# Keys and queries of the last six quads: transposed by DMA, scored in 64-row tiles

## The chip, the core and the metric

The kernel runs on one core of a Trainium2 chip. Its engines work beside each other and meet through semaphores: PE (matrix multiplies, with its weight loads listed as PEld), DVE (VectorE), ACT (ScalarE), POOL (GpSimd) and SP, which here issues DMAs only. POOL issues DMAs as well. The metric is the device time of one execution in microseconds. Before the change it is 323.39 us, the median of three runs (322.47 to 325.67).

## The reference

Attention with a decay per token, for 8 batches of 8 heads, 576 tokens, head dimension 64; its output is then put through a two-layer network with a tanh gelu.

```
scores = q @ k.T / sqrt(64)                      # per batch and head, 576 x 576
cum    = cumsum(log(clip(f, 1e-4, 1)))           # f: batch x head x token
attn   = softmax(where(causal, scores + cum_q - cum_k, -1e9))
x      = attn @ v      -> 4608 tokens x 512      # heads side by side
out    = gelu_tanh(x @ w_in) @ w_out             # 512 -> 2048 -> 512, float32 out
```

All inputs are float32 in HBM.

## The kernel before

**Quads.** Attention goes by quads of four heads of one batch: 16 quads, numbered i = 0 to 15, batch i // 2. Everything that belongs to quad i lies in buffer i % 2 of a pair. For a quad, `load_one` brings keys and queries from HBM with one DMA each, issued by POOL, which also makes bfloat16 of them (`k_c`, `q_c`: 32 partitions a head, each with 18 tokens of 64). `transpose_words` then has DVE transpose them in 32x32 blocks of 32-bit words, so that a word holds two neighbouring elements of the head dimension: `kT` and `qT` have 32 partitions for each of the four heads, and the two elements (c = 0, 1) side by side.

**Scores.** `scores(i, r)` makes round r (of three) of a quad's scores, transposed: keys on partitions, queries along the columns, only those at or under the diagonal. The 1536 columns of a quad are cut into pieces of 64 to 448 columns, seven over the three rounds. For each c, piece and head there is one matmul of 32 rows (half of the head dimension), so that four heads run abreast on four row tiles of PE; the second pass, c = 1, is added to the first. Two exponentials on ACT then write `pt`. `mask` (POOL) or `mask_by_product` (DVE) clears what lies above the diagonal.

**Products.** `denominators` (D) sums `pt` with the decay weights, `attn_out` (V) multiplies it by the weighted values `vw`; `make_vw` (VW) makes these from `v_nat`, which `load_v` (LV) brings by five DMAs from SP. The quotient goes to `xT`, the network's input.

**The network.** It goes by chunks of 512 tokens, nine of them, partly by schemes that save one of eight block products (`seven_in`, `seven_products`). Its matmuls fill PE between the steps of attention. Its results are stored from SP, from four staging buffers (`o_st`).

**Order.** There is no planner: the order is written out by hand. `setup()`, then the list `FRONT` (quads 0 to 6 and the first chunks), then `TABLES[c]` for c = 2 to 8, one stage each. Each word is one step: `S.q4.0` is `scores` of quad 2c + 4, round 0; `M`/`m` masks; `D`, `V`, `VW` as above; `cl` a small copy on POOL; `TK`, `TQ` transposes of keys and queries; `LK`, `LQ` their loads; `LV` the loads of values; `P`, `R` first-layer products, `F`, `f`, `O` second-layer ones by so many steps; `G`, `K`, `T` sums on DVE; `X`, `Y` change ACT's table. A step for a quad above 15 is left out. Each engine takes its instructions in this order and waits, in order, for what each one needs; the framework puts the waits in by what each instruction reads and writes. So a step that waits holds all later steps on the same engine, also DMAs that POOL or SP issues.

In stage c the scores made are those of quads 2c + 3 (three rounds) and 2c + 4 (three rounds, the last at the stage's end). Quads 10 and 11 are scored in stages 3 and 4, and the last, 15, in stage 6.

Lines of the profile that matter here: L191 the loads of keys and queries, L168 those of values, L197 DVE's transposes, L260 the score matmuls, L268 the exponentials, L274 POOL's masks, L214 `make_vw`, L219 `cl`, L328 the products D and V, L347 the first step after D, L359 `xT`, L540 and L373 matmuls of the network, L553 the stores.

Of the kernel before, what the change touches and what calls it, by code (L numbers as in the profile page):

```python
# [9 lines left out]
BF16 = mybir.dt.bfloat16  # L10
# [6 lines left out]
def kernel(  # L17
# [10 lines left out]
    nc = tc.nc  # L28

    B, H, S, D = q.shape  # L30
# [13 lines left out]
    NB = S // 64  # L44
# [42 lines left out]
    TABLES[2] = """  # L87
        Y O.512 P.0.1 R.1 P.4.1 R.1 R.1 TK.q3 TQ.q3 LK.q5 LQ.q5 m.q2.1 M.q2.2.2 m.q2.0 m.q2.2.3 CL.q2 LV P.2 G.0 P.3 K.3.0 K.3.1 K.3.2 P.6 P.7 K.3.3
        G.1.1.2 X F.10 S.q3.0 D.q2 M.q3.0 f.22 S.q3.1 V.q2.0 TK.q4 TQ.q4 M.q3.1 VW.q3 f.18 S.q3.2 V.q2.1 M.q3.2 cl.q3 TK.q5 f.16 S.q4.0 VW.q4 cl.q4
        D.q3 M.q4.0 f.18 S.q4.1 TQ.q5 V.q3.0 M.q4.1 f.13 V.q3.1 T f.3 S.q4.2  # L90
    """
    TABLES[3] = """
        Y O.512 LK.q4 LQ.q4 P.0.1 R.1 P.4.1 R.1 R.1 LK.q5 LQ.q5 M.q2.2 LV R.3 P.2.1 R.3 G.0.1.2 P.6 R.3 G.0.3.4 G.1.1.2 X F.10 S.q3.0 D.q2 M.q3.0
        f.22 S.q3.1 V.q2.0 TK.q4 TQ.q4 M.q3.1 VW.q3 f.18 S.q3.2 V.q2.1 M.q3.2 cl.q3 TK.q5 f.16 S.q4.0 VW.q4 cl.q4 D.q3 M.q4.0 f.18 S.q4.1 TQ.q5
        V.q3.0 M.q4.1 f.13 V.q3.1 T f.3 S.q4.2
    """
    TABLES[4] = """
        Y O.512 LK.q4 LQ.q4 P.0.1 R.1 P.4.1 R.1 R.1 LK.q5 LQ.q5 M.q2.2 LV R.3 P.2.1 R.3 G.0.1.2 P.6 R.3 G.0.3.4 G.1.1.2 X F.10 S.q3.0 D.q2 M.q3.0
        f.22 S.q3.1 V.q2.0 TK.q4 TQ.q4 M.q3.1 VW.q3 f.18 S.q3.2 V.q2.1 M.q3.2 cl.q3 TK.q5 f.16 S.q4.0 VW.q4 cl.q4 D.q3 M.q4.0 f.18 S.q4.1 TQ.q5
        V.q3.0 M.q4.1 f.13 V.q3.1 T f.3 S.q4.2  # L100
    """
    TABLES[5] = """
        Y O.512 LK.q4 LQ.q4 P.0.1 R.1 P.4.1 R.1 R.1 LK.q5 LQ.q5 M.q2.2 LV R.3 P.2.1 R.3 G.0.1.2 P.6 R.3 G.0.3.4 G.1.1.2 X F.10 S.q3.0 D.q2 M.q3.0
        f.22 S.q3.1 V.q2.0 TK.q4 TQ.q4 M.q3.1 VW.q3 f.18 S.q3.2 V.q2.1 M.q3.2 cl.q3 TK.q5 f.16 S.q4.0 VW.q4 cl.q4 D.q3 M.q4.0 f.18 S.q4.1 TQ.q5
        V.q3.0 M.q4.1 f.13 V.q3.1 T f.3 S.q4.2
    """
    TABLES[6] = """
        Y O.512 P.0.1 R.1 P.4.1 R.1 R.1 LK.q5 LQ.q5 M.q2.2 LV R.3 P.2.1 R.3 G.0.1.2 P.6 R.3 G.0.3.4 K.0.0 K.0.1 K.0.2 G.1.1.2 X F.10 S.q3.0 D.q2
        M.q3.0 f.22 S.q3.1 V.q2.0 M.q3.1 VW.q3 f.18 S.q3.2 V.q2.1 M.q3.2 cl.q3 f.20 D.q3 f.18 V.q3.0 v.q3.1 T f.14 K.0.3
# [17 lines left out]
    def many(n, shape, dtype, name):  # L127
        return [singles.tile(shape, dtype, name=f"{name}{i}") for i in range(n)]
# [57 lines left out]

    parts = [(0, QA), (QA, S)]

    def load_one(src, dst, i):
        b, h0 = i // QPB, 4 * (i % QPB)  # L190
        return nc.gpsimd.dma_start(  # L191
            out=dst[i % 2].rearrange("p a d -> p (a d)"),
            in_=src[b, h0:h0 + 4].rearrange("h (p a) d -> (h p) (a d)", p=32))

    def transpose_words(src, dst):

        nc.vector.transpose(  # L197
            out=dst.rearrange("p s c -> p (s c)").bitcast(FP32)
                .rearrange("p (t a) -> p a t", a=S // 32),
            in_=src.rearrange("p a d -> p (a d)").bitcast(FP32)  # L200
                .rearrange("p (a d) -> p a d", d=D // 2),
        )

    def transpose_k(i):
# [16 lines left out]
    def key_columns(i, key, h, c):  # L221

        b0 = {"low": 0, 0: 1, 1: 3, 2: 5, 3: 7, "high": NB}[key]
        return kT[i % 2][32 * h:32 * h + 32, 64 * b0:64 * b0 + 128, c]

    def load_exp():

        nc.scalar.activation(spare, shift[0:1, :], AF.Exp)
# [13 lines left out]
    def scores(i, r, groups=((0, 1, 2, 3),)):  # L242

        qq, p = qT[i % 2], pt[i % 2]
        if i < 2:
            off, n = split_rounds[r]
            todo = [(key, col - off, q0, nq) for (key, col, q0, nq) in split_pieces[r]]
        else:
            off, n = rounds[r]
            todo = []  # L250
            for (key, col, q0, nq) in pieces:
                a, z = max(col, off), min(col + nq, off + n)
                if a < z:
                    todo.append((key, a - off, q0 + a - col, z - a))
        for heads in groups:
            tiles = {g: psS.tile([128, 2, 512], FP32, name="ps_s", tag="s") for g in sorted({h // 2 for h in heads})}
            for c in range(2):
                for j, (key, c0, q0, nq) in enumerate(todo):
                    for h in heads:
                        nc.tensor.matmul(  # L260
                            tiles[h // 2][:, h % 2, c0:c0 + nq],
                            key_columns(i, key, h, c),
                            qq[32 * h:32 * h + 32, q0:q0 + nq, c],
                            start=(c == 0 and j == 0), stop=(c == 1),
                            skip_group_check=True,
                        )
            for g, t in tiles.items():
                nc.scalar.activation(p[:, 2 * g:2 * g + 2, off:off + n], t[:, :, 0:n], AF.Exp, scale=scale)  # L268
# [433 lines left out]
    def load_values(b, half):  # L702
# [124 lines left out]
```

## Time and profile before

The profiled execution took 322.39 us; the profile's span of it is 320.7 us. All durations below come from that one execution.

| | |
|---|---|
| median of three runs | 323.39 us |
| profiled execution / its span | 322.39 / 320.7 us |
| PE clock granted | full, all through |
| score matmuls (L260) | 896, in rounds of 16 or 24 |
| DVE transposes of keys and queries (L197) | 32, mean 1.24 us |
| loads of keys and queries (L191) | 32, 0.53 to 0.72 us of POOL each |
| stores (L553, from SP) | 35, median 2.3 us to landing |
| stage 3 / 4 / 5 | 132.3 to 166.0 / 166.0 to 199.6 / 199.6 to 233.3 us |

Idle time on an engine costs nothing unless another waits for it; where an engine is busy all the time, only its own work or what it waits for counts. A time of an instruction on POOL or SP that issues a DMA is the time to issue it; the transfer goes on after that ("to landing").

### The profile page before, as it was taken

Reading aid. Unit: us, or ns where it says so; the run is one execution under the profiler, and the core shown is the slowest. Engines: PE = TensorE matmul, PEld = TensorE weight load, DVE = VectorE, ACT = ScalarE, POOL = GpSimd, SP = SyncE. Lnnn points to the kernel's source line nnn. Section 1 sums busy time; section 2 is a strip of 40 time slices with the busy share of each in tenths; the row PEclk is TensorE's granted clock in tenths of the full one; section 3 lists DMA queues with packets and bytes.
Section 4 is the critical chain, followed back from the end, with each engine's and each line's share of the span. In section 5 each row is a group of like instructions: output and inputs, shape, how many; then the busy total and the mean of one; then the engine's idle time right before and its main releaser. Section 6 shows DMA issues by size and latency. Waiting matters only on the chain.

```text
span 320.7 us, 12340 instructions
## 1 busy us (share of the span) xinstructions
PE 312.5 (97%) x5522; PEld 218.9 (68%) x5542; DVE 249.8 (78%) x396; ACT 208.8 (65%) x264; POOL 112.4 (35%) x158
## 2 busy tenths in 40 slices
PE   8899999999999999999999999999999999999995
PEld 4457844545777577766777677768766788788784
DVE  4855159886779899788986898689878969886882
ACT  6985686766766686759756875778567844722730
POOL 8995454930500218600771068204710240000000
PEclk9999999999999999999999999999999999999999
DMA  7999999799103921692149512971120102003013
GB/s 126 226 179 208 209 233 210 148 192 209 37 4 112 174 40 37 133 221 45 37 94 196 113 37 67 170 163 37 35 70 0 37 32 72 3 34 100 0 35 98
DMA packets 47029, 33.45 MB, mean 104 GB/s; under 512 B 29824, under 2 KB 41216, under 8 KB 46976
## 3 DMA queue, kind: packets, MB, share of 16 engines
q0 software_dynamic: 9168, 15.99, 28.7%
q1 hardware_dynamic: 37664, 16.60, 19.7%
q8 instruction: 43, 0.70, 1.0%
q14 instruction: 10, 0.08, 0.1%
q10 hardware_dynamic: 144, 0.07, 0.1%
HBM read 36.85 MB, written 9.44 MB: 144 GB/s over the span
## 4 chain that ended last, share of the span: by engine, by line
PE 90%; DMA 6%; POOL 1%; issue 1%; DVE 1%; ACT 0%; POOLq 0%; DVEq 0%
PE ps_w L540 30%; PE ps_h L373 16%; PE po L328 10%; PE ps_cd L432 8%; PE ps_s L260 8%; PE ps_ab L432 6%; PE pso L610 4%; DMA w_in_sb<-in_moe_w_in_dram 3%; PE ps_h L490 3%; DMA q_c<-in_q_dram 2%; PE ps_h L387 2%; ACT pt L268 0%; PE ps_o L328 0%; POOL w_in_sb L180 0%; DVE qT L197 0%
## 5 line engine op out<-in xcount | busy, mean ns | idle before, releaser
L268 ACT ACTIVATE pt<-ps_s 128x1024 bf16<-128x1024 f32 (+2 forms) x100 | 94.0, 988 | 35.7 <-PE ps_s L260 32.0
L274 POOL TENSOR_SCALAR_AFFINE_SELECT pt<-pt 128x512 bf16<-128x512 bf16 (+2 forms) x67 | 41.1, 622 | 104.4 <-ACT pt L268 103.3
L373 PE MATMUL ps_h<-xT,w_in_sb 128*128 128x512 bf16 x228 | 54.5, 379 | 0.6
L540 PEld LDWEIGHTS <-gT 128*32 128x32 bf16 (+1 forms) x1247 | 50.6, 97 | 6.0 <-issue 1.7
L540 PE MATMUL ps_w<-w_out_sb,gT 128*32 128x256 bf16 (+1 forms) x1050 | 46.9, 273 | 0.0
L380 ACT ACTIVATE gT<-ps_h 128x1024 bf16<-128x1024 f32 x30 | 30.6, 1020 | 17.2 <-PE ps_h L373 16.7
L540 PEld LDWEIGHTS <-gsum 128*32 128x32 bf16 (+1 forms) x1256 | 39.3, 97 | 1.4
L373 PEld LDWEIGHTS <-w_in_sb 128*128 128x128 bf16 x240 | 23.4, 98 | 24.3 <-issue 0.4
L260 PE MATMUL ps_s<-qT,kT 32*128 32x64 bf16 (+5 forms) x896 | 36.6, 261 | 1.5 <-ACT pt L268 1.0
L214 POOL TENSOR_TENSOR vw<-v_nat,wT 128x1280 bf16<-128x1280 f32 (+1 forms) x13 | 29.5, 2266 | 4.9 <-DMA v_nat<-in_v_dram 4.4
L540 PE MATMUL ps_w<-usum,gsum 128*32 128x256 bf16 (+1 forms) x832 | 30.6, 273 | 0.0
L260 PEld LDWEIGHTS <-kT 32*128 32x128 bf16 x896 | 16.6, 92 | 18.9 <-issue 13.7
L197 DVE STREAM_TRANSPOSE kT<-k_c 128x576 f32<-128x576 f32 x16 | 19.9, 1245 | 11.0 <-DMA k_c<-in_k_dram 11.0
L441 ACT ACTIVATE gT<-snap 128x512 bf16<-128x512 f32 x45 | 26.1, 624 | 3.0 <-DVE snap L455 2.4
L565 DVE TENSOR_TENSOR o_st<-ps_w,snap 128x512 f32<-128x512 f32 x31 | 21.2, 685 | 8.4 <-PE ps_w L540 7.2
L432 PEld LDWEIGHTS <-w_in_sb 128*128 128x128 bf16 x240 | 23.4, 97 | 6.2 <-issue 1.5
L328 PE MATMUL po<-pt,vw 128*32 128x64 bf16 (+4 forms) x624 | 22.5, 278 | 0.0
L359 DVE TENSOR_TENSOR xT<-po,rb 128x576 bf16<-128x576 f32 x26 | 19.5, 751 | 3.6 <-PE po L328 3.0
L197 DVE STREAM_TRANSPOSE qT<-q_c 128x576 f32<-128x576 f32 x16 | 19.9, 1244 | 2.2 <-PE ps_s L260 1.7
L328 PEld LDWEIGHTS <-vw 128*32 128x32 bf16 x672 | 14.3, 97 | 10.3 <-issue 3.7
L432 PEld LDWEIGHTS <-xT 128*128 128x128 bf16 x180 | 17.6, 98 | 5.2
L432 PE MATMUL ps_cd<-xT 128*128 128x256 bf16 x120 | 18.0, 273 | 0.0
(105 smaller groups left out, 468.8 us busy)
## 6 DMA issues: line engine op xcount, KB each, us to landing
out_dram<-o_st SPq DMA_DIRECT2D x35, 256.0 KB, 2.3
k_c<-in_k_dram POOLq DMA_DIRECT2D x16, 288.0 KB, 5.7
q_c<-in_q_dram POOLq DMA_DIRECT2D x16, 288.0 KB, 6.8
v_nat<-in_v_dram SPq DMA_DIRECT2D x16, 256.0 KB, 6.8
v_nat<-in_v_dram SPq DMA_DIRECT2D x20, 128.0 KB, 5.0
w_out_sb<-in_moe_w_out_dram POOLq DMA_DIRECT2D x4, 512.0 KB, 10.8
v_nat<-in_v_dram POOLq DMA_DIRECT2D x9, 128.0 KB, 6.2
v_nat<-in_v_dram POOLq DMA_DIRECT2D x4, 256.0 KB, 7.3
```

What stands on the lines that cost most here:

```text
L197: nc.vector.transpose(out=dst.rearrange("p s c -> p (s c)").bitcast(FP32) .rearrange("p (t a) -> p a t", a=S // 32), in_=src.rearrange("p ...
L214: eng.tensor_mul(vw[i % 2][:, t0:t1], vb[:, t0:t1, h0:h0 + 4, :], wT[:, i, t0:t1, :].unsqueeze(3).to_broadcast([128, t1 - t0, 4, D]))
L260: nc.tensor.matmul(tiles[h // 2][:, h % 2, c0:c0 + nq], key_columns(i, key, h, c), qq[32 * h:32 * h + 32, q0:q0 + nq, c], start=(c == 0 an ...
L268: nc.scalar.activation(p[:, 2 * g:2 * g + 2, off:off + n], t[:, :, 0:n], AF.Exp, scale=scale)
L274: nc.gpsimd.affine_select(out=x, in_=x, compare_op=ALU.is_ge, fill=0.0, base=0, pattern=pattern, channel_multiplier=-1)
L328: nc.tensor.matmul(po[r0:r0 + w.shape[-1], 448 + q0:448 + q0 + nq], w, p[:, h, col:col + nq], start=(key in (0, "low")), stop=(key in ("lo ...
L373: nc.tensor.matmul(ph[:, j, :], w_in_sb[:, dt, 128 * ft:128 * ft + 128], xT[:, dt, CH * c:CH * (c + 1)], start=(dt == 0), stop=(dt == N_DT ...
L380: nc.scalar.activation(gT[:, 2 * pr:2 * pr + 2, :], ph, AF.Gelu_apprx_tanh)
L432: nc.tensor.matmul(ps[:, j], w[:, dt, 128 * j:128 * j + 128], x[:, dt], start=(first and j == 0 and dt == 0), stop=(dt == 1), skip_group_c ...
L441: nc.scalar.activation(gT[:, ft:ft + 2, HC * j:HC * (j + 1)], x, AF.Gelu_apprx_tanh)
L540: nc.tensor.matmul(ps[c0:c0 + width, n, cols[0]:cols[1]], x[:, j, 128 * n + c0:128 * n + c0 + width], w[:, j, cols[0]:cols[1]], start=(fir ...
L565: nc.vector.tensor_add(st, ps, kept[name])
```

## The change

From quad 10 on (`BY_DMA = 10`), keys and queries take another way; quads 0 to 9 keep theirs.

- `k_c` and `q_c` become the two halves of one tile, `kq`.
- A load brings tokens to partitions: for each head one DMA of 512 tokens (128 partitions by four blocks, 64 elements a run), and one for the last 64 tokens of all four heads. So a load is five DMAs from POOL, not one.
- Transposes are DMAs from SP, from SBUF to SBUF: for keys and queries of a quad two of 128x512 (two heads each) and one of 64x256 each, six a quad. DVE does none; it sets 64 columns of zeros once in each `kT` buffer.
- `kT` and `qT` hold the whole head dimension of one head on 64 partitions, two heads beside each other, the two pairs of heads one after the other along the columns. A score matmul has 64 rows and there is no second pass: two heads abreast, pair by pair.
- In the tables, loads of quads 10 to 15 move to the end of the stage before or to just before its attention part; transposes of the first quad move to the stage's start, before `LV`, and those of the second to just after `S.q3.2`.

```
     TABLES[2] = """
...
-        D.q3 M.q4.0 f.18 S.q4.1 TQ.q5 V.q3.0 M.q4.1 f.13 V.q3.1 T f.3 S.q4.2
+        D.q3 M.q4.0 f.18 S.q4.1 TQ.q5 V.q3.0 M.q4.1 LK.q6 LQ.q6 f.13 V.q3.1 T LK.q7 LQ.q7 f.3 S.q4.2
...
     TABLES[3] = """
-        Y O.512 LK.q4 LQ.q4 P.0.1 R.1 P.4.1 R.1 R.1 LK.q5 LQ.q5 M.q2.2 LV R.3 P.2.1 R.3 G.0.1.2 P.6 R.3 G.0.3.4 G.1.1.2 X F.10 S.q3.0 D.q2 M.q3.0
-        f.22 S.q3.1 V.q2.0 TK.q4 TQ.q4 M.q3.1 VW.q3 f.18 S.q3.2 V.q2.1 M.q3.2 cl.q3 TK.q5 f.16 S.q4.0 VW.q4 cl.q4 D.q3 M.q4.0 f.18 S.q4.1 TQ.q5
-        V.q3.0 M.q4.1 f.13 V.q3.1 T f.3 S.q4.2
+        Y O.512 TK.q4 TQ.q4 P.0.1 R.1 P.4.1 R.1 R.1 M.q2.2 LV R.3 P.2.1 R.3 G.0.1.2 P.6 R.3 G.0.3.4 G.1.1.2 LK.q6 LQ.q6 X F.10 S.q3.0 D.q2 M.q3.0
+        f.22 S.q3.1 V.q2.0 M.q3.1 VW.q3 f.18 S.q3.2 TK.q5 TQ.q5 V.q2.1 M.q3.2 cl.q3 f.16 S.q4.0 VW.q4 cl.q4 D.q3 M.q4.0 f.18 S.q4.1 V.q3.0 M.q4.1
+        f.13 V.q3.1 T LK.q7 LQ.q7 f.3 S.q4.2
...
-    q_c = many(2, [128, S // 32, D], BF16, "q_c")
-    k_c = many(2, [128, S // 32, D], BF16, "k_c")
+    kq = many(2, [128, 2 * S // 32 * D], BF16, "kq")
+    k_c, q_c = ([t_[:, S // 32 * D * n:S // 32 * D * (n + 1)].rearrange("p (a d) -> p a d", d=D) for t_ in kq] for n in range(2))
...
+    BY_DMA = 10
+
     def load_one(src, dst, i):
         b, h0 = i // QPB, 4 * (i % QPB)
+        if i >= BY_DMA:
+            x, n = src[b, h0:h0 + 4], 0 if dst is k_c else 1
+            for h in range(4):
+                z = 1024 * n + 512 * (h // 2)
+                nc.gpsimd.dma_start(
+                    out=kq[i % 2][:, z:z + 512].rearrange("p (t h d) -> p t h d", t=4, h=2)[:, :, h % 2],
+                    in_=x[h, 0:512].rearrange("(t p) d -> p t d", p=128))
+            return nc.gpsimd.dma_start(
+                out=kq[i % 2][64 * n:64 * n + 64, 2048:2304].rearrange("p (h d) -> p h d", h=4),
+                in_=x[:, 512:].rearrange("h p d -> p h d"))
...
+    def by_dma(i, n, dst, first, step):
+        for g in range(2):
+            nc.sync.dma_start(out=dst[:, first + step * g:first + step * g + 512].rearrange("p (a x) -> p a x", x=128),
+                              in_=kq[i % 2][:, 1024 * n + 512 * g:1024 * n + 512 * g + 512], transpose=True)
+        nc.sync.dma_start(out=dst[:, first:first + 2 * step].rearrange("p (a x) -> p a x", a=2)[:, :, 512:S],
+                          in_=kq[i % 2][64 * n:64 * n + 64, 2048:2304], transpose=True)
...
     def transpose_k(i):
+        if i >= BY_DMA:
+            if i < BY_DMA + 2:
+                nc.vector.memset(flat(kT[i % 2])[:, 64 + S:128 + S], 0.0)
+            return by_dma(i, 0, flat(kT[i % 2]), 64, S + 64)
         transpose_words(k_c[i % 2], kT[i % 2][:, 64:64 + S])

     def transpose_q(i):
+        if i >= BY_DMA:
+            return by_dma(i, 1, flat(qT[i % 2]), 0, S)
         transpose_words(q_c[i % 2], qT[i % 2])
...
-            for c in range(2):
+            if i >= BY_DMA:
+                for g, t in tiles.items():
+                    for j, (key, c0, q0, nq) in enumerate(todo):
+                        for x in range(2):
+                            nc.tensor.matmul(
+                                t[:, x, c0:c0 + nq], key_rows(i, key, 2 * g + x),
+                                flat(qq)[64 * x:64 * x + 64, S * g + q0:S * g + q0 + nq],
+                                start=(j == 0), stop=True, skip_group_check=True)
+            for c in range(2 if i < BY_DMA else 0):
```

`flat` gives a tile with its columns in one row; `key_rows` picks a piece's 128 keys of one head out of `kT`. Tables 4 and 5 change as table 3 does, and table 6 loses its two loads and their later places accordingly (its steps for quads above 15 are left out).

More of the change, by code (lines that the diff above doesn't have):

```diff
@@ L96 @@
     """
     TABLES[4] = """
-        Y O.512 LK.q4 LQ.q4 P.0.1 R.1 P.4.1 R.1 R.1 LK.q5 LQ.q5 M.q2.2 LV R.3 P.2.1 R.3 G.0.1.2 P.6 R.3 G.0.3.4 G.1.1.2 X F.10 S.q3.0 D.q2 M.q3.0
-        f.22 S.q3.1 V.q2.0 TK.q4 TQ.q4 M.q3.1 VW.q3 f.18 S.q3.2 V.q2.1 M.q3.2 cl.q3 TK.q5 f.16 S.q4.0 VW.q4 cl.q4 D.q3 M.q4.0 f.18 S.q4.1 TQ.q5
-        V.q3.0 M.q4.1 f.13 V.q3.1 T f.3 S.q4.2
+        Y O.512 TK.q4 TQ.q4 P.0.1 R.1 P.4.1 R.1 R.1 M.q2.2 LV R.3 P.2.1 R.3 G.0.1.2 P.6 R.3 G.0.3.4 G.1.1.2 LK.q6 LQ.q6 X F.10 S.q3.0 D.q2 M.q3.0
@@ L101 @@
+        f.22 S.q3.1 V.q2.0 M.q3.1 VW.q3 f.18 S.q3.2 TK.q5 TQ.q5 V.q2.1 M.q3.2 cl.q3 f.16 S.q4.0 VW.q4 cl.q4 D.q3 M.q4.0 f.18 S.q4.1 V.q3.0 M.q4.1
+        f.13 V.q3.1 T LK.q7 LQ.q7 f.3 S.q4.2
     """
     TABLES[5] = """
-        Y O.512 LK.q4 LQ.q4 P.0.1 R.1 P.4.1 R.1 R.1 LK.q5 LQ.q5 M.q2.2 LV R.3 P.2.1 R.3 G.0.1.2 P.6 R.3 G.0.3.4 G.1.1.2 X F.10 S.q3.0 D.q2 M.q3.0
-        f.22 S.q3.1 V.q2.0 TK.q4 TQ.q4 M.q3.1 VW.q3 f.18 S.q3.2 V.q2.1 M.q3.2 cl.q3 TK.q5 f.16 S.q4.0 VW.q4 cl.q4 D.q3 M.q4.0 f.18 S.q4.1 TQ.q5
@@ L105 @@
-        V.q3.0 M.q4.1 f.13 V.q3.1 T f.3 S.q4.2
+        Y O.512 TK.q4 TQ.q4 P.0.1 R.1 P.4.1 R.1 R.1 M.q2.2 LV R.3 P.2.1 R.3 G.0.1.2 P.6 R.3 G.0.3.4 G.1.1.2 LK.q6 LQ.q6 X F.10 S.q3.0 D.q2 M.q3.0
+        f.22 S.q3.1 V.q2.0 M.q3.1 VW.q3 f.18 S.q3.2 TK.q5 TQ.q5 V.q2.1 M.q3.2 cl.q3 f.16 S.q4.0 VW.q4 cl.q4 D.q3 M.q4.0 f.18 S.q4.1 V.q3.0 M.q4.1
+        f.13 V.q3.1 T LK.q7 LQ.q7 f.3 S.q4.2
     """
     TABLES[6] = """
-        Y O.512 P.0.1 R.1 P.4.1 R.1 R.1 LK.q5 LQ.q5 M.q2.2 LV R.3 P.2.1 R.3 G.0.1.2 P.6 R.3 G.0.3.4 K.0.0 K.0.1 K.0.2 G.1.1.2 X F.10 S.q3.0 D.q2
@@ L109 @@
-        M.q3.0 f.22 S.q3.1 V.q2.0 M.q3.1 VW.q3 f.18 S.q3.2 V.q2.1 M.q3.2 cl.q3 f.20 D.q3 f.18 V.q3.0 v.q3.1 T f.14 K.0.3
+        Y O.512 TK.q4 TQ.q4 P.0.1 R.1 P.4.1 R.1 R.1 M.q2.2 LV R.3 P.2.1 R.3 G.0.1.2 P.6 R.3 G.0.3.4 K.0.0 K.0.1 K.0.2 G.1.1.2 LK.q6 LQ.q6 X F.10
+        S.q3.0 D.q2 M.q3.0 f.22 S.q3.1 V.q2.0 M.q3.1 VW.q3 f.18 S.q3.2 TK.q5 TQ.q5 V.q2.1 M.q3.2 cl.q3 f.20 D.q3 f.18 V.q3.0 v.q3.1 T f.14 K.0.3
     """
@@ L202, in transpose_words, with flat @@
         )
+    def by_dma(i, n, dst, first, step):
[4 more added lines that the diff above has]
+                          in_=kq[i % 2][64 * n:64 * n + 64, 2048:2304], transpose=True)
+    def flat(t_):
+        return t_.rearrange("p s c -> p (s c)")
     def transpose_k(i):
+        if i >= BY_DMA:
+            if i < BY_DMA + 2:
+                nc.vector.memset(flat(kT[i % 2])[:, 64 + S:128 + S], 0.0)
+            return by_dma(i, 0, flat(kT[i % 2]), 64, S + 64)
         transpose_words(k_c[i % 2], kT[i % 2][:, 64:64 + S])
     def transpose_q(i):
+        if i >= BY_DMA:
+            return by_dma(i, 1, flat(qT[i % 2]), 0, S)
         transpose_words(q_c[i % 2], qT[i % 2])
@@ L224, in key_columns, with key_rows @@
         return kT[i % 2][32 * h:32 * h + 32, 64 * b0:64 * b0 + 128, c]
+    def key_rows(i, key, h):
+        b0 = {"low": 0, 0: 1, 1: 3, 2: 5, 3: 7, "high": NB}[key]
+        return flat(kT[i % 2])[64 * (h % 2):64 * (h % 2) + 64, (S + 64) * (h // 2) + 64 * b0:(S + 64) * (h // 2) + 64 * b0 + 128]
     def load_exp():
```

## The prediction

> **What bounds the kernel now.** I read the page first, then the waits, then the busy time by stage, and last the order of work on PE, POOL and SP in one stage. The page and the table of waits of the whole span:
>
> ```profile
> span 320.7 us, 12340 instructions
> PE 312.5 (97%) x5522; PEld 218.9 (68%) x5542; DVE 249.8 (78%) x396; ACT 208.8 (65%) x264; POOL 112.4 (35%) x158
> PE ps_s L260 <- ACT pt L268: 1.0, 3, 0.5
> PE ps_s L260 <- DVE qT L197: 0.5, 2, 0.4
> ```
>
> PE is busy nearly all the time, and the last two lines (who waited for whom: total, times, longest) are almost all that score matmuls ever wait for. A busy PE may still be a slow one, so I took the stages one by one. Stages 3, 4 and 5 of the loop, the ones that transpose quads 10 to 15:
>
> ```profile
> 132.30:166.00 33.70, 33.60 (x725) 24.37 (x727) 28.57 (x44) 23.93 (x30) 13.38 (x19) 1.00 0.49 104
> 166.00:199.60 33.60, 33.49 (x725) 24.21 (x726) 28.47 (x44) 23.93 (x30) 13.16 (x19) 1.00 0.51 105
> 199.60:233.30 33.70, 33.60 (x729) 24.34 (x728) 28.57 (x44) 23.93 (x30) 12.66 (x17) 1.00 0.49 104
> ```
>
> Columns: stretch, its length, then busy time of PE, weight loads, DVE, ACT, POOL, then the granted clock. The same three stages, 33.7 us each, PE without a gap at full clock; DVE has 5 us free in each and POOL 20. So only what changes PE's own matmuls or makes PE wait can change the time. POOL in stage 3 has work with a due time:
>
> ```profile
> 131.18 0.59 POOL L191 DMA_DIRECT2D k_c<-in_k_dram  x1
> 131.76 0.54 POOL L191 DMA_DIRECT2D q_c<-in_q_dram  x1
> 134.37 1.22 POOL L274 TENSOR_SCALAR_AFFINE_SELECT pt<-pt 128x512 bf16<-128x512 bf16 x2 [0.19 <-ACT pt L268]
> 151.65 1.14 POOL L274 TENSOR_SCALAR_AFFINE_SELECT pt<-pt 64x256 bf16<-64x256 bf16 x2 [16.06 <-ACT pt L268]
> 154.51 0.63 POOL L274 TENSOR_SCALAR_AFFINE_SELECT pt<-pt 128x512 bf16<-128x512 bf16 x1 [1.72 <-ACT pt L268]
> 155.11 2.33 POOL L214 TENSOR_TENSOR vw<-v_nat,wT 128x1280 bf16<-128x1280 f32 x1
> 157.77 1.22 POOL L274 TENSOR_SCALAR_AFFINE_SELECT pt<-pt 128x512 bf16<-128x512 bf16 x2 [0.33 <-ACT pt L268]
> ```
>
> and PE at the same time:
>
> ```profile
> 147.89 0.69 PE L260 MATMUL ps_s<-qT,kT 32*128 32x64 bf16 x24
> 148.51 0.87 PE L328 MATMUL po<-pt,w_bf 128*32 128x512 bf16 x24
> 149.20 2.58 PE L540 MATMUL ps_w<-w_out_sb,gT 128*32 128x256 bf16 x88
> 151.71 0.63 PE L260 MATMUL ps_s<-qT,kT 32*128 32x64 bf16 x16
> 158.77 0.87 PE L328 MATMUL po<-pt,w_bf 128*32 128x512 bf16 x24
> ```
>
> The last masks of quad 9 end at 158.99 and the denominators D of quad 9 start at 158.77, reaching the first column that these masks wrote after 1024 columns. At the rate of the ps_w row (88 matmuls of 256 columns, four abreast, in 2.51 us: 0.445 ns a column) that is 0.46 us, at 159.2. That is the narrow place: 0.2 us of slack.
>
> **PE's own work.** Six quads of seven pieces by four heads need one matmul each instead of two: 168 matmuls and 168 weight loads fewer. But four 32-row tiles abreast become two 64-row tiles abreast: a first round streams 576 columns twice either way, the others 512 twice. The rounds take 0.62, 0.56 and 0.56 us (start of ps_s to start of the next group), of which 0.51, 0.46 and 0.46 is streaming at 0.445 ns. No row has a 64-row tile. Bounds over the 18 rounds: -1.9 us if all that isn't streaming vanished (6 x 0.31), +8.6 if pairs ran singly (6 x 1.43). Nearest is the four-tile row itself, with the same groups and switches to and from other tilings: I take 0.
>
> **DVE.** Twelve transposes of 1.245 us go, 14.9 us in all; two small memsets come. PE waits for none of this in stages 3 to 5, so the gain is 0.
>
> **Loads on POOL.** Each of twelve loads (0.55 us of POOL) becomes four of 512 runs and one of 256. The nearest rows are the value loads from POOL, with as many runs of 256 bytes:
>
> ```profile
> L168 SPq DMA_DIRECT2D v_nat<-in_v_dram x40: 409/844/4001, 50.3 to 212.0; - x40
> L168 POOL DMA_DIRECT2D v_nat<-in_v_dram x15: 625/769/922, 4.7 to 50.7; - x15
> ```
>
> (min/median/max in ns.) So 4 x 0.769 + 0.625 = 3.70 us a load, 7.4 a quad instead of 1.1. The low bound is today's 0.55 a DMA, the high one 0.92. Quads 10 and 11 are now loaded at the end of stage 2, 12 and 13 in stage 3, 14 and 15 in stage 4, ahead of masks in POOL's order. Stage 2 to 3: from 131.18, two quads take 14.8 us, to 146.0. Queued behind them are the masks of quad 8's last round, 1.22 us, done at 147.2; PE asks for them 0.46 us into 148.51, so they hold, with 1.7 us. Next come quad 12's loads, 7.4 us, to 154.6, and behind them 1.14 + 0.63 + 2.33 + 1.22 = 5.32 us of masks and weighted values: 159.9, against 159.2. PE waits 0.7 us, and all that follows with it.
>
> The next stages have more room. In stage 4 the loads of quad 13 (kT's other buffer) start when M.q4.1 ends, 32.7 us into stage 3, and end some 7.4 us later, 6.5 us into stage 4. Masks 1.2 and quad 14's loads 7.4 then end at 15 us, before the masks' exponentials (19.4). Stage 5 loads nothing.
>
> Each load also takes one of eight semaphores in turn, so the ninth waits for the landing of the first. Eight issues take 5.9 us and the value loads of this size landed after 6.2 (median, in the page's DMA issues): 0.3 us a round of eight, 0.7 with the 28 loads before the masks of quad 9.
>
> **Transposes on SP.** Six DMAs a quad, four of 128x512 and two half as large at most, 12 a stage in stages 3 to 5. They are queued ahead of the value loads and, for the second quad, between the stores. SP's row gives 0.41 us for a value load that meets no other traffic and 4.0 for one that does (median 0.84): these are my bounds for a large one; nothing shows a transpose. I take 1.5, above the median, since POOL's loads now move at the same time. Four large and two half-size make 5 x 1.5 = 7.5 us a quad, 15 a stage; value loads add about 9 to 10 and stores 1.6. That is 26 of 33.7 us: SP isn't the bound. The first quad's have from 2.2 us (the store ahead of them) to 25.9 (its first scores) and the second's some 26 us. Value loads slip by 7 us and delay the second weighted-values product on POOL, whose reader comes a stage later; a store slips by a few us, with four o_st buffers a stage apart. Cover gone: quad 14's loads wait for quad 12's transposes. With b for a large one these end at 2.6 + 5b + about 2.5 to land, and POOL then has two more us of loads, which must be over by 21.5 (the 19.4 above and the 1.72 + 0.33 us that POOL idles before its next masks): b up to 2.9 costs nothing.
>
> [...]
>
> **Sum.** 0 for PE and DVE, +0.7 on POOL, +0.7 for semaphores of loads: about +1.2 to 1.4. The profiled execution took 322.39 us (span 320.7 and 1.7 around it), so 323.7; the median of the runs is 1.0 above it, so about 324.6.
>
> **Rivals.** (B) Loads land late. The key and query loads of today land after 4.0 to 13.4 us, and at the start of each stage 12 transposes, value loads and these share the DMA engines, whose busy share is at or near 1.0 in such stretches already (202 to 206 us). At 8 us of landing, POOL waits 2 us at the ninth and at the seventeenth load, so that the masks of quad 8 end at 151.3 instead of 147.2 and miss 148.97 by 2.4; quad 12's loads add another 2 us, and the masks of quad 9 miss their time by 4.5 on top: +7, 330. From 7 to 10 us of landing it is +3 to +12.
> (C) SP becomes the bound, from b above 2.9. At the 4.0 us of the contended row SP needs 40 + 11 = 51 us a stage, 17 too many, 52 over three, less the 23 of slack: +29, 353. For it: the second and third value loads of stages 3 to 5 held SP 3 to 4 us while POOL's loads moved. Against: in stage 2, without that traffic, all five took 0.4 to 1.2.
> (D) No change: a load costs POOL 0.6 or less (today's 0.55 for a DMA with cast), 151.65 is met with room and nothing waits: 323.4.
> (E) The pairs of 64-row tiles run one after the other: +8.6, 332. Against: four 32-row tiles do run abreast.
> (F) Faster: DVE held PE after all, in delays too short for the table of waits; if a quarter of its 14.9 us shows, -3.7, 319.7 (a quarter is my choice: less would not be told from no change). Against: three stages of 33.7 us with no gap, each matmul one column time after the last.
>
> **Numbers.** Forecast 0.42, D 0.13, B 0.22, C 0.15, E 0.03, F 0.05. One per cent, 3.2 us, is about what a measurement tells from no change. Same: forecast and D, 0.55; slower: B, C, E, 0.40; faster: F, 0.05. The range runs from just under D's time, 322, to 335, near the end of B: it leaves out F and C, 0.2.
>
> **What would show it.** Right: PE's score rounds of quads 10 to 15 at 0.56 to 0.62 us with 12 and 8 matmuls; stages 4 and 5 at 33.7 us; stage 3 longer by about one, with PE waiting for pt from POOL in the denominators of quad 9; POOL's loads at 0.77 us. B: waits of POOL for landings and PE waiting in quad 8's denominators too. C: SP issues of over 2.9 us, PE waiting for qT or kT from DMA. E: rounds near 1.0 us. Wrong altogether: stages 3 to 5 shorter than 33.7.

## The result and the profile after

The changed kernel takes 326.78 us (median of 20 runs, 323.5 to 338.38) against 323.03 for the kernel before, run beside it: a ratio of 1.0098, 95% interval 1.0077 to 1.0119. It is 1% slower. The forecast was 324.6, a change too small to be told from none; the time lies inside its range, but the kernel is slower by more than the interval. In four of the twenty executions the mean granted clock was 0.957 to 0.977, against 0.993 to 1.000 in the others, and the time 330 to 338 us: the ratios leave such executions out, and of experiments that were profiled in one only the part from stage 3 on is read. The profiled execution of the changed kernel took 327.8 us, 1.0 above its median.

From the page of the changed kernel, the span, PE, and two DMA queues (packets, megabytes, share of 16 engines):

```profile
span 326.1 us, 12170 instructions
...
PE 315.2 (97%) x5374; PEld 219.3 (67%) x5374; DVE 238.4 (73%) x386; ACT 208.6 (64%) x264; POOL 148.8 (46%) x206
...
q0 software_dynamic: 36048, 16.00, 41.6%
...
q8 instruction: 42, 0.69, 0.9%
```

DVE is relieved and POOL loaded, as they were meant to be. q0, the queue of POOL's loads, moves the megabytes it moved before (15.99) in four times the packets (9168 before), and takes 41.6% of the engines' time instead of 28.7%. The last line is the instructions themselves: the page counts their 42 packets among those of the same 16 DMA engines. The three stages that the prediction read:

```profile
132.30:166.00 33.70, 30.12 (x551) 21.00 (x552) 21.14 (x36) 21.55 (x28) 31.58 (x43) 0.95 1.59 144
166.00:199.60 33.60, 33.60 (x682) 24.35 (x674) 24.54 (x40) 23.87 (x30) 23.75 (x32) 1.00 1.05 130
199.60:233.30 33.70, 33.70 (x684) 24.39 (x678) 24.64 (x40) 23.87 (x30) 18.65 (x25) 1.00 0.89 121
```

The second and third are full. The first has lost 3.6 us of PE's time and some of its clock (0.95, third figure from the end). What PE waited for, in the table of waits of the whole span:

```profile
PE ps_w L581 <- issue: 2.9, 1, 2.9
...
PE po L369 <- issue: 0.7, 1, 0.7
PE po L369 <- DVE xT L400: 0.5, 1, 0.5
```

"issue" means that no semaphore held PE. The first two stops lie in stage 3 and the third in stage 6. PE's timeline in stage 3:

```profile
151.79 0.84 PE L369 MATMUL po<-pt,vw 128*32 128x512 bf16 x20
153.34 0.21 PE L369 MATMUL po<-pt,vw 128*32 128x64 bf16 x4 [0.71 <-issue]
...
156.70 0.50 PE L581 MATMUL ps_w<-usum,gsum 128*32 128x256 bf16 x12
160.08 1.83 PE L581 MATMUL ps_w<-usum,gsum 128*32 128x256 bf16 x44 [2.88 <-issue]
...
162.27 1.14 PE L294 MATMUL ps_s<-qT,kT 64*128 64x64 bf16 x12
163.34 1.30 PE L369 MATMUL po<-pt,w_bf 128*32 128x512 bf16 x24
```

PE halts in the midst of one row of matmuls, which waited for no semaphore, by 0.95 us (start to start) among quad 8's output products and by 3.15 us among the weights of the network. The score round after it takes 1.14 us, where the same round takes 0.67 in stage 4. That is the clock, in the busy time by stretch (the granted clock is the third figure from the end, the DMA engines' busy share, which goes above 1 in such stretches, the one behind it):

```profile
160.00:161.66 1.66, 1.58 (x45) 1.51 (x48) 0.00 (x0) 0.00 (x0) 1.51 (x3) 0.76 0.80 163
161.66:163.40 1.74, 1.74 (x31) 0.70 (x24) 0.69 (x1) 0.37 (x1) 1.68 (x2) 0.50 0.72 88
163.40:165.00 1.60, 1.60 (x46) 1.01 (x48) 0.29 (x1) 1.57 (x2) 0.25 (x1) 0.72 0.11 22
```

Together these come to 3.4 us at half clock, which start 0.8 us after PE goes on.

And POOL, whose row of work the prediction had followed:

```profile
131.62 3.06 POOL L197 DMA_DIRECT2D kq<-in_k_dram  x4 [0.88 <-DVE o_st L606]
...
145.89 1.60 POOL L315 TENSOR_SCALAR_AFFINE_SELECT pt<-pt 128x512 bf16<-128x512 bf16 x2
147.46 3.00 POOL L197 DMA_DIRECT2D kq<-in_k_dram  x4
...
154.35 0.63 POOL L200 DMA_DIRECT2D kq<-in_q_dram  x1
154.98 1.87 POOL L315 TENSOR_SCALAR_AFFINE_SELECT pt<-pt 64x256 bf16<-64x256 bf16 x3
156.82 2.33 POOL L242 TENSOR_TENSOR vw<-v_nat,wT 128x1280 bf16<-128x1280 f32 x1
159.11 1.22 POOL L315 TENSOR_SCALAR_AFFINE_SELECT pt<-pt 128x512 bf16<-128x512 bf16 x2
```

The last masks of quad 9 end at 160.3 (forecast 159.9 plus up to 0.7), but PE comes for them only after 163.3: its own stop hides their lateness.

**Where the time went.** From the start of quad 8's last score round (131.65 before, 131.16 after) to PE's last matmul (316.99 and 322.14), PE takes 185.3 us before and 191.0 after: 5.6 more. The stop at 153 is 0.9, that at 160 is 3.15, the rounds at half clock behind it 1.45, and 0.5 comes in stage 6. The 18 score rounds give 0.02 us each back, 0.4. The ratio stands for 3.2 us only. The half clock is part of the difference: the profiled execution had a mean granted clock of 0.993, but ten of the sixteen executions behind the ratio had 0.998 or more, and 3.4 us at half clock would alone have taken 0.005 off (1.7 of 326 us). So these ten did without it.

**Blocks of instructions.** In the trace a packet of the instruction queue that feeds PE has 16,384 bytes, and there is one for every 256 of PE's instructions (matmuls, weight loads and a few waits, counted from the start; 42 for 10,765 in the changed kernel). The edge of a block is the number of instructions ahead of it. From stage 3 on, every stop of PE over 0.35 us that no semaphore explains, in this and the later profiles, falls at 193 + 256 n of these, at an edge. The distance is that of PE from the edge, in instructions, when the packet starts (up to 20 too large in the kernel before, whose trace lacks 20 matmuls). The last four rows are of experiments told below:

```
kernel             edge   packet runs       PE's distance to   PE stops and
                   at     (us)              the edge then      goes on (us)
before             5057   149.12 - 150.45   263                -
before             5313   152.77 - 153.96   271                -
changed            5057   150.87 - 152.03   85                 152.38 - 153.34
changed            5313   157.06 - 158.57   0                  156.93 - 160.08
one load           5057   152.33 - 153.21   73                 153.68 - 154.92
late values        5569   158.02 - 159.32   133                159.87 - 160.75
no transposes      5057   157.76 - 158.64   221                -
no transposes      5313   161.71 - 162.59   213                -
```

PE goes on 1.3 to 1.7 us after the packet's end. So, by an estimate from these rows, a packet has to start 2.2 to 3.2 us ahead of PE, with its own 0.9 to 1.5 us; that is met where it starts nearly a whole block ahead, as in the kernel before. In the changed kernel it started late; the packets themselves took 1.2 and 1.5 us, against 1.3 and 1.2 before.

### The profile page after: what moved, and what is told of

Read it like the earlier page. It is cut to its first block, busy times and chain, and to the rows that moved or that the text cites. A ratio compares the mean times of both kernels' runs of the same rounds, so it can differ in the third digit from the quotient of the medians.

```text
span 326.1 us, 12170 instructions
## 1 busy us (share of the span) xinstructions
PE 315.2 (97%) x5374; PEld 219.3 (67%) x5374; DVE 238.4 (73%) x386; ACT 208.6 (64%) x264; POOL 148.8 (46%) x206
## 3 DMA queue, kind: packets, MB, share of 16 engines
q0 software_dynamic: 36048, 16.00, 41.6%
## 4 chain that ended last, share of the span: by engine, by line
PE 90%; DVE 4%; DMA 2%; issue 2%; POOL 1%; ACT 0%; POOLq 0%; DVEq 0%
PE ps_w L581 28%; PE ps_h L414 16%; PE po L369 9%; PE ps_cd L473 8%; PE ps_ab L473 6%; PE ps_s L301 6%; PE pso L651 4%; PE ps_h L531 4%; PE ps_s L294 3%; DMA kq<-in_q_dram 2%; PE ps_h L428 2%; PE po_m L355 1%; DVE xT L400 1%; DVE gsum L566 1%; POOL kq L203 0%
## 5 line engine op out<-in xcount | busy, mean ns | idle before, releaser
L315 POOL TENSOR_SCALAR_AFFINE_SELECT pt<-pt 128x512 bf16<-128x512 bf16 (+2 forms) x67 | 40.3, 613 | 70.9 <-ACT pt L309 69.6
L242 POOL TENSOR_TENSOR vw<-v_nat,wT 128x1280 bf16<-128x1280 f32 (+1 forms) x13 | 30.5, 2344 | 4.3 <-PE ps_s L301 3.9
L301 PE MATMUL ps_s<-qT,kT 32*128 32x64 bf16 (+5 forms) x560 | 24.7, 261 | 1.6 <-ACT pt L309 1.2
L301 PEld LDWEIGHTS <-kT 32*128 32x128 bf16 x560 | 11.3, 92 | 13.8 <-issue 9.3
L209 DVE STREAM_TRANSPOSE kT<-kq 128x576 f32<-128x576 f32 x10 | 12.5, 1248 | 10.9 <-DMA kq<-in_k_dram 10.9
L197 POOL DMA_DIRECT2D kq<-in_k_dram x24 | 18.2, 779 | 2.6 <-DMA kT<-kq 1.4
L197 POOL DMA_DIRECT2D kq<-in_q_dram x24 | 18.1, 808 | 0.3 <-DMA kq<-in_k_dram 0.3
```

The source lines that it names most:

```text
L197: nc.gpsimd.dma_start(out=kq[i % 2][:, z:z + 512].rearrange("p (t h d) -> p t h d", t=4, h=2)[:, :, h % 2], in_=x[h, 0:512].rearrange("(t ...
L242: eng.tensor_mul(vw[i % 2][:, t0:t1], vb[:, t0:t1, h0:h0 + 4, :], wT[:, i, t0:t1, :].unsqueeze(3).to_broadcast([128, t1 - t0, 4, D]))
L301: nc.tensor.matmul(tiles[h // 2][:, h % 2, c0:c0 + nq], key_columns(i, key, h, c), qq[32 * h:32 * h + 32, q0:q0 + nq, c], start=(c == 0 an ...
L315: nc.gpsimd.affine_select(out=x, in_=x, compare_op=ALU.is_ge, fill=0.0, base=0, pattern=pattern, channel_multiplier=-1)
```

## The experiments

Theory: the transposes, ahead of the value loads on SP, push these into PE's attention part, and the DMA traffic there delays PE's blocks. Rival: POOL's order alone (the forecast's late masks), or the fine loads alone. "Before" in a ratio is the kernel before, run beside it.

**One part at a time.** The 64-row scores stay in all three.

```
     def load_one(src, dst, i):
-        if i >= BY_DMA:
+        if False:
...
     def transpose_k(i):
-            return by_dma(i, 0, flat(kT[i % 2]), 64, S + 64)
+            return None
...
     def transpose_q(i):
-            return by_dma(i, 1, flat(qT[i % 2]), 0, S)
+            return None
```

The first edit alone, with transposes of what then lies in the tile:

> Quads 10 to 15 are loaded by one DMA each for keys and queries, as quads 0 to 9 are, at the places of the changed kernel; the transposes by DMA and the 64-row score matmuls stay. The data are then laid out wrongly, so the scores of these quads aren't those of the reference. Theory 'collision' (PE stands still in stage 3 because its instructions come late, while transposes from SP and the fine loads from POOL crowd the DMA engines): no crowd, so no stop; what is left is the gain seen in the score rounds, 18 times about 0.025 us: -0.4 against before, 322.6. Rival 'POOL order' (masks of quad 9 late behind the loads): the same, since POOL has 1.1 us a quad instead of 7.4. Rival 'transposes' (the transposes alone hold DMA traffic up): stays near the changed kernel, +3, 326.

Ratio 1.0096 (1.0061 to 1.0132). With coarse loads the long stop is gone and the one at edge 5057 stays, 1.24 us: the time is that of the rival "transposes", and the crowd of fine loads isn't needed for a stop.

The other two alone:

> The twelve transposes of keys and queries of quads 10 to 15 from SP are left out (their scores use what an earlier quad left in the buffers); the fine loads from POOL and the 64-row score matmuls stay. 'Collision': no stop of PE for instructions, but POOL still reaches the masks of quad 9 some 1.5 us late, so +1 against before, 324.0, with PE waiting for pt in the denominators of quad 9. 'POOL order' as the whole cause: unchanged, +3, 326. 'Transposes': -0.4. A further rival, that the fine loads alone (128-byte runs) crowd the DMA engines: PE still stops without a semaphore in stage 3, +3.

Ratio 1.0132 (1.0083 to 1.018). No stop without a semaphore, as "collision" had it, but the time is that of "POOL order": PE waits 2.6 us for POOL's masks instead, 0.7 of it already in quad 8's denominators. POOL itself waited 1.2 us for landings of earlier loads there, which is rival B's sign, in small.

All three:

> From quad 10 on each load is one DMA of whole rows instead of five of single heads, and the transposes aren't issued at all, so the keys and queries of quads 10 to 15 are not the reference's; the 64-row scores, the order of the steps and the relief of VectorE stay. Theory (PE's blocks of instructions, 16 KB each, come late when the loads and transposes still fill the DMA engines while PE goes through quads 8 and 9): with both gone no block is late, no stop of PE without a semaphore over 0.3 us in quads 8 and 9, masks of quad 9 on time; what is left is the faster score rounds (-0.4) and the 0.5 us in stage 6, so 0 to +0.3 us on the kernel before, ratio 0.999 to 1.002. Rival (the 64-row scores themselves slow PE, or the order of the steps does): +2 us or more, ratio from 1.006 up.

Ratio 1.0005 (0.9987 to 1.0024). From stage 3 on PE waits for nothing but 0.5 us in stage 6. In the second half of stage 3, PE's busy time (second figure) fills the stretch:

```profile
149.00:166.00 17.00, 17.00 (x566) 13.15 (x560) 11.70 (x20) 11.98 (x14) 10.75 (x14) 1.00 0.11 35
```

In the changed kernel the same stretch has 13.42 us of PE at 0.90 of the clock and 1.57 in place of the 0.11, the DMA engines' share. So scores and order cost nothing; either new transfer alone, placed as it is, costs about 1%, and both together 1% too. They don't add up; where both hold PE in the same place, it waits for the later of the two.

**Blocks, without anything of the change.** The kernel before, with its value loads later (stages 3 to 5):

```
-        ... M.q2.2 LV R.3 ... f.22 S.q3.1
+        ... M.q2.2 R.3 ... f.22 LV S.q3.1
```

> The kernel before, complete, with one thing moved: in stages 3 to 5 the loads of the values for the next batch element are issued after the score rounds of quad 9 have begun (at about 153 us) instead of at 134. No transposes by DMA, no fine loads, no 64-row scores. Theory (late blocks of instructions when DMA traffic meets quads 8 and 9): one or more stops of PE without a semaphore between 150 and 166 us, 0.5 to 3 us in sum, and the instruction packets after nominal 4972 come up to 200 instructions later than in the kernel before; ratio 1.002 to 1.01. Stages 4 and 5 show none, if the blocks are only scarce in stage 3. Rival (the stops belong to the transposes or to the 128-byte packets): no stop, ratio 0.998 to 1.002.

Ratio 1.0034 (1.0019 to 1.0048). PE's timeline in stage 3:

```profile
159.21 0.94 PE L540 MATMUL ps_w<-w_out_sb,gT 128*32 128x256 bf16 x28
160.75 0.95 PE L540 MATMUL ps_w<-w_out_sb,gT 128*32 128x256 bf16 x28 [0.60 <-issue]
```

Stops of 0.87, 0.83 and 0.49 us, in stages 3, 4 and 5, all at edges (5569, 7105, 8385; the table of waits puts the third down to a copy on POOL, whose result these matmuls don't read). Theory held, with stages 4 and 5 not excepted. No transpose is needed and no packet of 128 bytes. Nor does the crowd on the DMA engines decide by itself. These are the stretches ahead of the late packet of edge 5569 in this run, and ahead of the packet of edge 5313 in the run without transposes, which was not late (the DMA engines' share is the last figure but one):

```profile
156.20:158.00 1.80, 1.80 (x76) 1.57 (x68) 1.80 (x3) 1.25 (x2) 1.47 (x2) 1.00 1.31 250
159.70:161.70 2.00, 2.00 (x72) 1.25 (x66) 2.00 (x4) 0.94 (x2) 2.00 (x4) 1.00 1.38 88
```

The shares are alike. The first is traffic of SP, the second of POOL. SP's values moved in 256-byte packets, some 900 a us, around every late packet of the table but one; at 157.06, values, transposes and fine loads moved together. POOL's loads alone made no packet late in this part of the stage. So lateness goes with traffic that SP issues, though such traffic isn't always enough: in the kernel before, the packet of edge 7873 starts at 214.44, a whole block ahead, while values move at the same pace.

**Fewer instructions.** Stage 3's `f` (four 32-column tiles) became `F` (one wide matmul), in the changed kernel and, as its control, in the kernel before.

> All computed as in the changed kernel; in stage 3 the second-layer matmuls of the previous chunk between the steps of attention run as whole 128-column tiles instead of four 32-column tiles abreast: a quarter of the instructions for the same streaming. 'Collision' with late instructions: the crowd on the DMA engines stays, but PE needs a third of the instructions there and doesn't run out: the 3.7 us stop goes, and what stays is POOL's lateness, 1 to 2 us, plus switches between tilings (no row for these; under 0.1 us for each of about 12): +1 to +3 less than the changed kernel's own +3.1. 'POOL order': not faster than the changed kernel, with PE waiting for pt.

Ratio 1.0135 (1.0108 to 1.0163); no stop without a semaphore in stages 3 to 5. In its place, in quad 9's denominators:

```profile
161.87 0.31 PE L369 MATMUL po<-pt,w_bf 128*1 128x320 bf16 x4 [0.66 <-POOL pt L315]
162.46 0.28 PE L369 MATMUL po<-pt,w_bf 128*1 128x192 bf16 x8 [0.29 <-POOL pt L315]
```

Start to start that is 0.97 and 0.55 us too long: 1.5 us, the forecast's own term, uncovered. Both causes are real, one behind the other.

> The kernel before, complete, with stage 3's output products in wide matmuls: the control for the two runs with wide matmuls. Theory: PE's time is the columns it passes, so nothing within 0.4 us, ratio 0.998 to 1.002. Rival (a wide product leaves less for the waits of attention to fall between, or takes the banks of PSUM for longer): +1 us or more, ratio from 1.003.

Ratio 1.002 (1.0 to 1.004): wide matmuls may cost 0.6 us by themselves. They may account for a part of the 4.4 us that the run with wide matmuls lost. From quad 8's last round on its profile is 2.3 us longer than that of the kernel before; the rest isn't found in a part that was changed, and stays open. The 0.1 us for a switch between tilings, in the expectation, was the author's estimate: no run shows a switch alone, and the control's interval, 0 to 1.3 us, is for all that the wide matmuls cost, switches among it.

**POOL's order.** Loads of quads 12 and 14 from ahead of the masks to behind `M.q4.1`:

> All computed as in the changed kernel; in stages 3 and 4 the loads of quads 12 and 14 move from before the stage's attention part to after M.q4.1, beside those of quads 13 and 15, as stage 2 has it. 'Collision': the transposes of quad 11 (153 to 164 us) then meet no loads, and later collisions fall where PE runs wide matmuls and needs few instructions: no stop, -0.4 to +0.5, about 323.0. 'POOL order': POOL is through its loads before the masks of quad 9, so the same -0.4 to 0. 'Transposes': +3.

Ratio 1.011 (1.0075 to 1.0146): a miss. Masks were on time, but the stops at 5057 and 5313 stayed (1.5 and 0.4), and the loads pushed the masks at the head of stage 4 from 177.0 to 181.1, into a sum of DVE (lines from the timeline):

```profile
181.08 1.40 POOL L315 TENSOR_SCALAR_AFFINE_SELECT pt<-pt 128x512 bf16<-128x512 bf16 x2
181.16 1.88 DVE L560 TENSOR_TENSOR gsum<-gT 128x1024 bf16<-128x1024 bf16 x1
```

The sum takes 0.68 alone. ACT then started its exponentials 1 us later in the stage, and PE waited 0.5 us for them.

> The changed kernel without the transposes by DMA (so quads 10 to 15 have other queries and keys than the reference) and with the loads of quads 12 and 14 behind the masks of quad 10 or 12 on POOL; the fine loads and the 64-row scores stay. Theory (fine loads alone cost POOL's time, through late masks, and the stops of PE without a semaphore need the transposes too): masks on time and no such stop over 0.5 us from 149 to 200 us; what is left is 0.5 us in stage 6 less 0.4 of the score rounds, ratio 0.999 to 1.003. Rival (128-byte packets alone hold PE's blocks up): stops without a semaphore of 1 us or more in stage 3 or 4, ratio from 1.005 up.

Ratio 1.0053 (1.0027 to 1.0079), above the theory's 1.003 and at the rival's lower end. Its profiled execution took 1781 us and can't tell which it was.

> The changed kernel, complete, with three things at once: stage 3's output products in wide matmuls (fewer instructions while the DMA engines are full), the loads of quads 12 and 14 behind the masks of quad 10 or 12, and the scores block by block over both pairs of heads. Theory (instruction blocks and POOL's order bound the stage one behind the other, and each hides the other, so that one repair alone gains little): stage 3 on, PE takes 185 to 186.5 us from the first score round of quad 8's predecessor to its end, as in the kernel before (185.3); ratio 0.998 to 1.004. Rival (the repairs add nothing to one another, as wide matmuls or later loads alone): ratio from 1.008 up.

Ratio 1.0103 (1.0049 to 1.0158), PE 188.4 us from quad 8's last round on: a miss. No stop at an edge, no late mask, but 2.0 us of waits for ACT's exponentials in stages 3 to 5. Later loads alone gave 0.5 of such waits, wide matmuls alone none; what makes the rest isn't shown.

So the loads were spread: none in stage 3 between the masks of quads 8 and 10, and those for quads 13 and 15 behind the masks that open their stage.

```
 TABLES[3], [4]:  -  G.1.1.2 LK.q6 LQ.q6 X ... M.q4.1 ... T LK.q7 LQ.q7 f.3
                  +  G.1.1.2 X ... M.q4.1 LK.q6 LQ.q6 ... T f.3
 TABLES[4], [5]:  -  M.q2.2 LV
                  +  M.q2.2 LK.q5 LQ.q5 LV
```

> The changed kernel, complete, with the loads spread so that POOL has none between the masks of quad 8's last round and those of quad 10, and so that the masks at the head of stage 4 don't slip behind loads: quads 12 and 14 after the masks of quads 10 and 12, quads 13 and 15 after the masks that open their stage; scores block by block over both pairs. Theory: masks on time, no wait of PE for ACT in stages 4 and 5, nothing in stage 6; left are the stops without a semaphore in stage 3 (1.2 to 2 us, as with the later loads alone) less 0.4 of the score rounds: +0.8 to +1.6 us on the kernel before, ratio 1.002 to 1.006. Rival (stops move on to stage 4, where the loads now stand): +2 to +4 us, ratio 1.007 to 1.012.

Ratio 1.004 (1.0009 to 1.0072). All that PE waits for from stage 3 on:

```profile
PE po L369 <- issue: 0.4, 1, 0.4
PE ps_w L581 <- issue: 0.2, 1, 0.2
```

Start to start, 0.7 and 0.4 us at 5057 and 5313, and 0.5 at 7873.

> As the run with the loads spread, but the transposes by DMA aren't issued (quads 10 to 15 have other queries and keys than the reference): the fine loads alone, well placed. Theory (a stop needs the transposes, or the values that they push back): no stop of PE without a semaphore over 0.5 us from stage 3 on, no late mask; the score rounds' 0.4 us is all that is left, ratio 0.997 to 1.001. Rival (128-byte packets alone hold up PE's blocks): stops of 0.5 us or more, ratio from 1.004.

Ratio 0.9995 (0.9972 to 1.0018), and PE waits for nothing from stage 3 on. So the fine loads, well placed, are free; what is left in the kernel with spread loads, 1.5 us, goes with the transposes.

**SP's order.** The values ahead of the transposes:

```
-        Y O.512 TK.q4 TQ.q4 ... M.q2.2 LV R.3
+        Y O.512 LV TK.q4 TQ.q4 ... M.q2.2 R.3
```

> The changed kernel, complete, with the loads of the values put ahead of the transposes in SP's order in stages 3 to 5, so that they go at 132 to 142 us as in the kernel before; the transposes of quad 10 come behind them. Theory: the block of instructions at nominal 4794 to 5042 comes on time, the 0.9 us stop at the first output products of quad 8 is gone; the stop of 3.1 us among the weights of quad 9, which falls with quad 12's fine loads and quad 11's transposes, can stay; between -0.9 and -4 us on the changed kernel, ratio to before 0.998 to 1.007. Rival (POOL's order alone sets the loss): as the changed kernel, ratio 1.008 to 1.012.

Ratio 1.0271 (1.0213 to 1.0328): a bad miss. Who waited for whom, for PE from stage 3 on, then for POOL from 150 to 182 us:

```profile
PE po L369 <- POOL pt L315: 7.4, 9, 2.5
...
POOL kq L197 <- DMA kT<-kq: 3.8, 2, 2.4
```

The transposes now ended at 159.7, and quad 12's loads, on POOL ahead of quad 9's masks, wait until they free the buffer. The prediction had named this chain ("quad 14's loads wait for quad 12's transposes"). Here its cover was gone. The stops at 5057 (1.30) and 5313 (0.68) were there too, so the theory failed as well: the transposes now moved where the values had.

> The changed kernel, complete, with three things undone: the values ahead of the transposes (stages 3 to 5), the loads of quads 12 and 14 behind the masks of quad 10 or 12 on POOL (stages 3 and 4), and the scores of a round written block by block over both pairs of heads instead of pair by pair. Theory: both stops in stage 3 and POOL's lateness gone, and stage 6's 0.5 us too; what is left is the faster score rounds, so -0.4 to +0.5 us on the kernel before, ratio 0.998 to 1.002. Rival (transposes cost PE their time wherever they lie): +2 us or more, ratio from 1.006 up.

Ratio 1.0099 (1.0068 to 1.013): a miss. The transposes took the values' place in time, and the stop at 5057 stayed (1.1), with 0.4 at 5313, 0.7 at 7873, and waits for masks.

**Stage 6.** Pieces in the outer loop, pairs of heads in the inner one:

```
-                for g, t in tiles.items():
-                    for j, (key, c0, q0, nq) in enumerate(todo):
+                for j, (key, c0, q0, nq) in enumerate(todo):
+                    for g, t in tiles.items():
```

> The changed kernel, complete, with only the scores of a round written block by block over both pairs of heads instead of pair by pair. Theory (the first pair's exponentials come 0.25 us earlier, and POOL's product of values and weights then meets VectorE's sum in stage 6): the gap of 0.75 us at the second output product of quad 14 goes to 0.25 or less, stage 3 stays as slow as it is; -0.4 to -0.6 us on the changed kernel, ratio to before 1.006 to 1.010. Rival (the gap belongs to the 64-row scores or to chance): gap stays at 0.75, ratio 1.008 to 1.012.

Ratio 1.0081 (1.0044 to 1.0118). The changed kernel in stage 6 (timelines of POOL, DVE, PE):

```profile
259.97 0.63 POOL L315 TENSOR_SCALAR_AFFINE_SELECT pt<-pt 128x512 bf16<-128x512 bf16 x1 [1.46 <-ACT pt L309]
260.00 1.15 DVE L566 TENSOR_TENSOR gsum<-gT,gsum 128x1024 bf16<-128x1024 bf16 x1
261.87 0.87 PE L369 MATMUL po<-pt,vw 128*32 128x512 bf16 x24 [0.55 <-DVE xT L400]
```

and with the other order:

```profile
266.77 1.17 POOL L315 TENSOR_SCALAR_AFFINE_SELECT pt<-pt 128x512 bf16<-128x512 bf16 x1 [1.50 <-ACT pt L309]
266.76 0.68 DVE L566 TENSOR_TENSOR gsum<-gT,gsum 128x1024 bf16<-128x1024 bf16 x1
268.17 0.87 PE L369 MATMUL po<-pt,vw 128*32 128x512 bf16 x24
```

Pair by pair, the first pair's exponentials come earlier, POOL's mask starts 0.03 us ahead of DVE's sum, the sum takes 1.15 us, and PE waits 0.55 us behind it. The other way round DVE is first by 0.01 us, the sum takes 0.68 and the mask 1.17, for which nobody waits. The stops of stage 3 came again, 0.98 and 3.15 us, at the same two edges.

**The split.** By the ratios, of the 3.2 us (0.98% of 323) some 0.5 is the order of the scores (1.0098 to 1.0081), 1.3 the place of the loads (to 1.0040), 1.5 the transposes and what they push back (to 0.9995). With these intervals each is uncertain by 1.3 to 1.6 us, so the ratios alone show only that the whole is lost and regained. The profiles say it more sharply, one execution each. From quad 8's last round on, PE takes 191.0 us in the changed kernel and 190.3 with the other order of scores (both with the half clock in them), 186.5 with the loads spread, 185.0 without the transposes; the kernel before takes 185.3, and scores and order alone 185.5. No version came out ahead of the kernel before, and the two without transposes, which leave out work that is needed, only equal it. So placing the transfers better had nothing to win here.

## Why the prediction was wrong

- **PE's own work (0): right.** The rounds take 0.60 and 0.54 us where the forecast had 0.56 to 0.62; 0.4 us gained, within its bounds. Pairs don't run singly (E).
- **DVE (0): right**, 11 us less busy and nothing gained (F).
- **Loads on POOL (+0.7, and +0.7 for semaphores): right in mechanism and near in size.** A load issue took 0.77 to 0.80 us (so not D), quad 12's ended at 154.98 (forecast 154.6), POOL waited 0.33 us for a landing, and with wide matmuls the wait shows: 1.5 us against 1.4. Without the transposes it was 2.6, as landings held POOL for longer there. In the changed kernel a longer stop hid it.
- **Transposes on SP (free up to 2.9 us each): the size right, the conclusion wrong.** SP's rows (count, then min/median/max in ns):

```profile
L218 SPq DMA_TRANSPOSE kT<-kq x12: 1190/1257/2115, 135.9 to 229.0; - x12
L218 SPq DMA_TRANSPOSE qT<-kq x12: 1188/1206/2174, 140.6 to 233.8; - x12
```

  1.2 us (median) against the 1.5 taken, so SP wasn't the bound (C); the transposes landed after 4.2 us (median). What failed is the sentence "Value loads slip by 7 us and delay the second weighted-values product on POOL, whose reader comes a stage later". On SP in stage 3, first before, then after:

```profile
134.91 9.02 SPq L168 DMA_DIRECT2D v_nat<-in_v_dram  x5
...
144.93 6.12 SPq L168 DMA_DIRECT2D v_nat<-in_v_dram  x5
...
152.96 4.39 SPq L218 DMA_TRANSPOSE kT<-kq  x2
```

  The values slipped by 10 us, and I asked only who reads the values, not what else their traffic meets. In the kernel before, the values had landed by 146.4, before PE's attention part begins at 147.9. Now they, and the second quad's transposes, moved during it: PE's blocks came late and PE stood still for 0.95 and 3.15 us.
- **"So only what changes PE's own matmuls or makes PE wait can change the time": right, but the list of what makes PE wait was incomplete.** The page before listed the instruction queue (43 packets); I took PE's instructions for granted.
- **Stage 6 (not in the sum): missed**, 0.5 us.
- **Rival B** (late landings, +3 to +12) came near in size and was another mechanism: landings of loads held POOL 0.33 us in all in the changed kernel and 1.2 without the transposes, not 2 for every eight loads.
- **Order of size:** forecast +1.2, measured 3.2. Its 1.4 on POOL is there; the sum lacked the blocks and the clash in stage 6.

## What to carry over

When transfers move, ask what they meet as well as who reads them: PE's instructions came over the same DMA engines here, one packet per 256, and where PE ran small matmuls it ate a block in 3.6 to 3.8 us (kernel before, edges 5057 to 5825), so here SP's bulk traffic is better over by then. A stop of PE inside one row of matmuls, with "issue" as its cause, is to be checked against the instruction queue. Two causes that end at the same time hide each other, so a repair that gains nothing alone may still be needed, and the order of a queue is to be checked for what each move pushes behind it.

## What the hardware showed

- **Late blocks.** What in an SP transfer delays a block's packet stays open; at the same share of the DMA engines, 1.3 to 1.4, POOL's loads delayed none. In the kernel before, PE didn't stop at edges 5057 and 5313, whose packets started 263 and 271 instructions ahead of it; where SP's transfers ran beside small matmuls, it stopped for 0.4 to 3.15 us an edge.
- **The clock.** After the 3.15 us stop the granted clock was 0.50 for 3.4 us, from 0.8 us after PE went on, worth 1.45 us; after stops of 1.24 us (one load) and 1.5 us (later loads) it stayed at 1.00. What brings it on, and what sets its length, isn't shown.
- **DVE and POOL.** A sum of DVE between two bfloat16 tiles took 1.15 and 1.88 us instead of 0.68 when a mask of POOL had started 0.03 and 0.08 us earlier; where the sum was first by 0.01, the mask took 1.17 instead of 0.63. In each of these rows the second took 0.1 us less than what the first had left and its own time alone (in the row of 1.88 us, the first was two masks). The cause isn't shown.
- **Transposes by DMA** took SP the same 1.2 us for 128x512 and for 64x256 (1.18; medians, 24 and 12 of them).
- **Packets.** One of 128 bytes in POOL's loads took 32 ns (median of 27,648), one of 2304 bytes 192: three times as long per byte, which is where the rise of that queue's share comes from.
